# Two later starts: pieces six and seven of w_out are converted at slices 40 and 48 of the first product

## The chip, the cores and the metric

The kernel runs on one core of a Trainium2 chip. Its engines are TensorE (PE; its weight loads are PEld), VectorE (DVE), ScalarE (ACT), GpSimd (POOL) and SyncE (SP), which only issues transfers here. Each engine works through its own instructions in the order in which the program emits them. The metric is the device time of one execution in microseconds; lower is better.

## The reference, cut to what matters

Three stages follow each other for 2 batches of 768 tokens:

```python
# 1: retention, 8 heads of 64
state = gamma * state + k_t v_t^T ;  y_t = scale * q_t @ state
# 2: a gated feed-forward block, d_model 512, d_ff 1024
h = np.maximum(x @ w_in, 0.0)
conv_out = sum(conv_w[k] * hp[:, k:k + S, :] for k in range(3))
x = h * sigmoid(conv_out) @ w_out
# 3: eight experts, one for each token, chosen from logits
logits = x @ w_gate ;  out = p[e] * (relu(x @ w1[e]) @ w2[e])
```

All weights and activations of stage 2 count as float32, but `w_in`, `w_out` and `conv_w` arrive as 64-bit floats. The kernel reads them as pairs of 32-bit words and builds the float32 values itself.

## The kernel before, in words

**Precision.** A float32 product is done as three TensorE products in the faster fp32r form (`mm3`, lines 133 to 135): high part by high part, high by low, low by high. Each operand is therefore split into a high and a low part first.

**Conversion of a weight piece** (`convert`, line 160, with `narrow`, line 146). The matrix w_in comes in eight pieces of 128 x 512 and w_out in eight more, numbered m = 0 to 7. Called wo6 and wo7 here are the last two. One piece goes through these steps:

- SP issues the load of the raw words (line 143), long before the rest.
- DVE shifts and masks the high words (line 149, `na<-raw`) and merges two bits (line 150); ACT scales the low words (line 151, `raw<-raw`).
- POOL adds the two as integers (line 153, `na<-na,raw`).
- ACT writes the high part (line 174, `woh`), DVE the low part (line 176, `wol`).
- For w_out alone: TensorE turns the piece (line 185, `wt_ps`), ACT copies it (line 189, `wt`), TensorE multiplies it with the gate weights (line 193, `wc_ps`, only 9 columns wide), ACT stores that (line 195, `wc`).

`convert` is a generator. Each `yield n` says after how many further calls of `advance()` (line 409) it goes on, so it spreads over the work around it. A piece with an entry in `GATES` (line 157) waits ahead of its narrowing until the counter `slices[0]` has reached the entry.

**The product with w_in.** `stream(0, range(8))` emits, for each of eight blocks m of 128 features and each half u of the tokens, four slices of one `mm3` each (`ffn_in`, line 364): 64 slices, numbered from 0, so slices 0 to 7 are block 0, slices 32 to 39 block 4, slices 40 to 47 block 5. Its sum stands in a PSUM bank, `h_ps`, 128 x 384. After the fourth slice ACT applies the relu into a buffer `h` (line 376), which frees the bank. Slices 0 to 19 lie between chunks of stage 1; for slices 20 to 63 one `advance()` runs per slice:

```python
    psa = pool("psa", 3, q_stack, space=PSUM)
    ...
    for _ in first:
        slices[0] += 1
        advance()
```

That pool of three banks, handed out in turn, serves `h_ps` and from here on also `wc_ps`. So a `wc_ps` or an `h_ps` waits until the bank handed out three requests earlier has been read by ACT.

**The block chain** (`hidden`, line 346). A finished block m then goes, at fixed distances in slices (`TIMES`, line 381), through ACT `cc<-h,cw` (line 350), two DVE taps (line 353), the ACT sigmoid (line 355), a DVE product (line 357), the ACT high part `hg` (line 326), the DVE low part (line 330), and TensorE's logit products (`lg`, line 344), which also need the stored `wc` of the piece with the same number. Below, h3 is the chain of block 3, and so on.

The order of every engine's queue thus follows from these counts. ACT, for example, meets the relu of a block only after all that was emitted before it, whatever that waits for.

**Afterwards** batch 1 takes the same product, then the products with w_out (`x_ps`), the routing, and the experts with their weight loads; these stages use what was converted above.

Of the kernel before, what the change touches and what calls it, by code (L numbers as in the profile page):

```python
# [91 lines left out]
def tile_kernel(ctx, tc, cat, cst, qT, kT, kN, vN, w_in, conv_w, w_out, wg, w1, w2, out):  # L92
# [61 lines left out]
        yield 2  # L154
        return a.bitcast(F32)

    GATES, slices = {6: 34, 7: 44}, [0]
    turning, held, loaded, ready, banks = [], [], [], [], [0]

    def convert(src, hi, lo, m=None):  # L160
# [902 lines left out]
```

## Time and profile before

| what | value |
|---|---|
| runs shown, device us | 436.66, 432.30, 436.14; median 436.14 |
| profiled execution: device time | 432.95 us |
| profiled execution: span | 431.2 us |
| granted TensorE clock, mean | 0.99 of full speed |
| busy: PE, DVE, ACT, POOL | 95%, 67%, 60%, 21% of the span |
| PE busy, 85 to 135 us | 48.20 of 50.00 us, granted clock 0.97 |
| PE busy, 135 to 250 us | 112.23 of 115.00 us, granted clock 1.00 |

The span runs from the first to the last instruction. Matmuls are pipelined, so one lasts longer than the distance to the next one; distances between starts say what a stretch of TensorE work costs. A releaser in square brackets is the instruction whose end ended a wait.

### The profile page before, as it was taken

The numbers are of one execution on the slowest core, as the hardware profiler recorded it, in microseconds if no ns is written. First come the engines' busy times: TensorE is split into PE (matmuls) and PEld (weight loads), VectorE is DVE, ScalarE is ACT, GpSimd is POOL, SyncE is SP. The second block draws the span as 40 slices with busy tenths as digits, with TensorE's granted clock in tenths as the row PEclk, the third lists the DMA queues.
The fourth block names the chain that finished last, engine by engine and source line by source line (L and its number), as shares of the span: only waits on it lengthen the run. The fifth ranks groups of instructions, "written<-read, shape, count | busy, mean of one in ns | idle before, by whom it ended". The sixth has DMA issues, their size and how long they took to land.

```text
span 431.2 us, 7291 instructions
## 1 busy us (share of the span) xinstructions
PE 408.8 (95%) x2412; PEld 329.2 (76%) x2412; DVE 289.6 (67%) x518; ACT 259.2 (60%) x429; POOL 91.5 (21%) x92
## 2 busy tenths in 40 slices
PE   8898999999899999999999999999999999999991
PEld 7787897899798778988768776867738677776880
DVE  3798789787767260377899058968664796858650
ACT  2787677667666212566704166869556686958560
POOL 5256664211110000000000330305203132211210
PEclk9999999999899999999999999999999999999997
DMA  7989763230000101000197899999969999774100
GB/s 229 388 291 398 260 211 92 93 97 1 2 0 2 49 26 49 26 0 2 58 377 254 304 373 379 342 390 409 398 254 340 407 364 346 280 260 186 44 25 29
DMA packets 27324, 86.59 MB, mean 201 GB/s; under 512 B 3598, under 2 KB 4622, under 8 KB 27280
## 3 DMA queue, kind: packets, MB, share of 16 engines
q1 hardware_dynamic: 25200, 79.76, 50.4%
q0 software_dynamic: 2080, 6.29, 3.9%
q8 instruction: 21, 0.34, 0.3%
q14 instruction: 23, 0.19, 0.1%
HBM read 105.18 MB, written 6.55 MB: 259 GB/s over the span
## 4 chain that ended last, share of the span: by engine, by line
PE 35%; issue 26%; DMA 15%; DVE 14%; ACT 4%; POOL 3%; SPq 1%; POOLq 0%; DVEq 0%; ACTq 0%
DMA out_dram<-yo,it 13%; PE h_ps L133 5%; PE h_ps L134 4%; PE h_ps L135 4%; PE x_ps L133 4%; PE x_ps L134 3%; PE x_ps L135 3%; PE y L300 3%; DVE cc L353 3%; PE s_ps L282 2%; POOL xg L727 2%; PE inc L290 1%; DMA kq<-in_qT_dram 1%; PE y L302 1%; DVE na L149 1%
## 5 line engine op out<-in xcount | busy, mean ns | idle before, releaser
L133 PE MATMUL h_ps<-xT,wih 128*128 128x384 f32 x128 | 46.9, 366 | 0.0
L353 DVE SCALAR_TENSOR_TENSOR cc<-h,cw,cc 128x768 f32<-128x768 f32 x32 | 34.4, 1075 | 18.6 <-ACT cc L350 18.5
L863 POOL DMA_INDIRECT out_dram<-yo,it x13 | 16.7, 1282 | 136.3 <-ACT yo L862 136.3
L727 POOL DMA_INDIRECT xg<-xs,it x13 | 18.8, 1444 | 123.4 <-DMA qc<-in_w_dram 115.8
L134 PE MATMUL h_ps<-xT,wih 128*128 128x384 f32 x128 | 43.5, 340 | 0.0
L135 PE MATMUL h_ps<-xT,wil 128*128 128x384 f32 x128 | 43.4, 339 | 0.0
L133 PE MATMUL x_ps<-woh,hg 128*128 128x512 f32 x96 | 38.5, 401 | 0.0
L134 PE MATMUL x_ps<-wol,hg 128*128 128x512 f32 x96 | 37.6, 391 | 0.0
L135 PE MATMUL x_ps<-woh,hg 128*128 128x512 f32 x96 | 37.5, 391 | 0.0
L718 DVE TENSOR_TENSOR ws0l<-r,ws0l 128x1024 fp32r<-128x1024 f32 x22 | 26.0, 1221 | 16.3 <-ACT ws0l L717 16.2
L153 POOL TENSOR_TENSOR na<-na,raw 128x512 int32<-128x512 int32 (+1 forms) x17 | 21.9, 1289 | 48.9 <-ACT raw L151 17.7
L300 PE MATMUL y<-at,vz 128*128 128x128 f32 x192 | 30.6, 281 | 1.8 <-ACT vz L277 0.9
L718 DVE TENSOR_TENSOR ws0h<-r,ws0h 128x1024 fp32r<-128x1024 f32 x22 | 26.0, 1221 | 8.2 <-ACT ws0h L717 8.2
L718 DVE TENSOR_TENSOR wc<-r,wc 128x1024 fp32r<-128x1024 f32 x22 | 25.9, 1221 | 8.0 <-ACT wc L717 8.0
L717 ACT ACTIVATE ws0l<-r 128x1024 fp32r<-128x1024 f32 x22 | 22.1, 1052 | 13.9 <-PE y L135 13.9
L282 PE MATMUL s_ps<-qz,kq 128*128 128x256 f32 x96 | 29.2, 386 | 1.0 <-issue 1.0
L718 DVE TENSOR_TENSOR ws1h<-r,ws1h 128x1024 fp32r<-128x1024 f32 x22 | 26.0, 1221 | 6.0 <-ACT ws1h L717 3.8
L717 ACT ACTIVATE wc<-r 128x1024 fp32r<-128x1024 f32 x22 | 22.1, 1054 | 11.3 <-PE g L135 11.3
L300 PEld LDWEIGHTS y<-at,vz 128*128 128x128 f32 x192 | 25.4, 191 | 4.3 <-DVE xT L305 2.3
L284 DVE TENSOR_TENSOR at<-s_ps,ca 128x256 f32<-128x256 f32 x48 | 20.2, 420 | 11.7 <-PE s_ps L282 11.6
L133 PEld LDWEIGHTS h_ps<-xT,wih 128*128 128x128 f32 x128 | 24.6, 192 | 3.1 <-issue 1.8
L489 ACT ACTIVATE xn<-x_ps 128x512 f32<-128x512 f32 x10 | 6.0, 599 | 32.8 <-PE x_ps L135 18.2
(231 smaller groups left out, 1044.9 us busy)
## 6 DMA issues: line engine op xcount, KB each, us to landing
r<-in_w_dram SPq DMA_DIRECT2D x88, 512.0 KB
qc<-in_w_dram SPq DMA_DIRECT2D x32, 512.0 KB
qs1l<-in_w_dram SPq DMA_DIRECT2D x32, 512.0 KB
raw<-in_w_in_dram SPq DMA_DIRECT2D x8, 512.0 KB
raw<-in_w_out_dram SPq DMA_DIRECT2D x8, 512.0 KB
kq<-in_qT_dram SPq DMA_DIRECT2D x7, 384.0 KB
kq<-in_kT_dram SPq DMA_DIRECT2D x7, 384.0 KB
kv<-in_vN_dram SPq DMA_DIRECT2D x7, 384.0 KB
```

The source lines that it names most:

```text
L133: te.matmul(ps, lhi, rhi, start=first, stop=False)
L134: te.matmul(ps, lhi, rlo, start=False, stop=False)
L135: te.matmul(ps, llo, rhi, start=False, stop=last)
L153: po.tensor_tensor(out=a, in0=a, in1=lo, op=ALU.add)
L282: te.matmul(ps, self.kq[:, 0, tok], self.qz[:, :, tok], start=True, stop=True)
L284: ve.tensor_tensor(out=self.at[c], in0=ps, in1=self.dm, op=ALU.mult)
L300: te.matmul(y, vz[:, c, j, :], at[:, j, :], start=(j == 0), stop=(c == 0 and j == 1))
L353: ve.scalar_tensor_tensor(out=cc, in0=h[:, i:i + S], scalar=cw[:, m, i:i + 1], in1=cc, op0=ALU.mult, op1=ALU.add)
L717: se.activation(out=w[:, 0, h, :], in_=r, func=AF.Copy)
L718: ve.tensor_tensor(out=w[:, 1, h, :], in0=r, in1=w[:, 0, h, :].bitcast(F32), op=ALU.subtract)
L727: return po.indirect_dma_start(out=xg, out_offset=None, in_=xs[0:n], in_offset=bass.IndirectOffsetOnAxis(ap=it[:, j:j + 1], axis=0), bound ...
L863: po.indirect_dma_start(out=out, out_offset=bass.IndirectOffsetOnAxis(ap=it[:, j:j + 1], axis=0), in_=yo, in_offset=None, bounds_check=NT ...
```

## The change

One line is changed. It sets from which slice on pieces 6 and 7 of w_out may be narrowed; their loads, their steps and the number of calls between the steps are as they were.

```diff
-    GATES, slices = {6: 34, 7: 44}, [0]
+    GATES, slices = {6: 40, 7: 48}, [0]
```

The line that reads it, in `convert`, is unchanged:

```python
        while slices[0] < GATES.get(m, 0):
            yield 1
```

## Rows read from the trace of the kernel before

**Rows 1.** Chain of waits, 80 to 140 us: start, time (us), engine, tile, line.

```profile
105.69 0.43 DVE na L149
106.14 0.69 DVE na L150
106.84 0.87 DVE cc L357
107.70 1.98 DVE cc L353
109.71 0.84 ACT cc L355
110.55 0.52 ACT woh L174
111.07 0.39 ACT h L376
```

**Rows 2.** TensorE timeline: start, us, engine, line, operation, tiles, count [idle, releaser].

```profile
100.34 0.34 PE L135 MATMUL h_ps<-xT,wil 128*128 128x384 f32 x1
...
101.72 0.42 PE L133 MATMUL h_ps<-xT,wih 128*128 128x384 f32 x1
...
103.42 0.44 PE L133 MATMUL h_ps<-xT,wih 128*128 128x384 f32 x1
...
104.74 0.34 PE L134 MATMUL h_ps<-xT,wih 128*128 128x384 f32 x1
...
109.60 0.34 PE L135 MATMUL h_ps<-xT,wil 128*128 128x384 f32 x1
...
111.50 1.35 PE L193 MATMUL wc_ps<-wgs,wt 128*128 128x9 f32 x8 [1.57 <-ACT h L376]
...
113.46 0.67 PE L133 MATMUL h_ps<-xT,wih 128*128 128x384 f32 x1
...
115.71 0.34 PE L134 MATMUL h_ps<-xT,wih 128*128 128x384 f32 x1
...
130.56 0.45 PE L133 MATMUL h_ps<-xT,wih 128*128 128x384 f32 x1
```

**Rows 3.** Busy time by window: us; PE, PEld, DVE, ACT, POOL; granted clock; DMA.

```profile
110.00:111.40 1.40, 0.00 (x0) 0.00 (x0) 0.84 (x2) 1.40 (x3) 0.00 (x0) 1.00 0.00 0
111.40:113.40 2.00, 1.90 (x12) 1.90 (x13) 1.34 (x3) 1.23 (x4) 0.00 (x0) 0.68 0.00 0
113.40:115.50 2.10, 2.10 (x8) 2.10 (x8) 2.10 (x4) 0.60 (x1) 0.00 (x0) 0.50 0.00 0
120.00:131.00 11.00, 11.00 (x81) 9.89 (x80) 8.22 (x10) 7.49 (x14) 0.53 (x1) 1.00 0.01 1
```

**Rows 4.** DVE timeline, the first tap of h3 and a later product.

```profile
104.75 1.02 DVE L353 SCALAR_TENSOR_TENSOR cc<-h,cw,cc 128x768 f32<-128x768 f32 x1 [0.86 <-ACT cc L350]
...
122.70 0.95 DVE L357 TENSOR_TENSOR cc<-cc,h 128x768 f32<-128x768 f32 x1
```

**Rows 5.** POOL timeline, the adds of wo6 and of wo7.

```profile
107.09 1.76 POOL L153 TENSOR_TENSOR na<-na,raw 128x512 int32<-128x512 int32 x1 [8.13 <-DVE na L150]
118.13 1.51 POOL L153 TENSOR_TENSOR na<-na,raw 128x512 int32<-128x512 int32 x1 [9.27 <-ACT raw L151]
```

**Rows 6.** Groups by line, 102 to 131 us: busy us, mean ns; idle, releasers.

```profile
L330 DVE TENSOR_TENSOR hg<-cc,hg 128x768 fp32r<-128x768 f32 x5 | 4.8, 955 | 1.2 <-ACT hg L326 1.2
L376 ACT ACTIVATE h<-h_ps 128x384 f32<-128x384 f32 x9 | 4.3, 482 | 4.0 <-PE h_ps L135 4.0
L326 ACT ACTIVATE hg<-cc 128x768 fp32r<-128x768 f32 x5 | 4.2, 844 | 3.9 <-DVE cc L357 3.9
L350 ACT ACTIVATE cc<-h,cw 128x768 f32<-128x768 f32 x4 | 3.7, 933 | 0.1
L189 ACT ACTIVATE wt<-wt_ps 128x512 f32<-128x512 f32 x4 | 2.2, 586 | 0.8 <-PE wt_ps L185 0.8
L151 ACT ACTIVATE raw<-raw 128x512 int32<-128x512 uint32 x2 | 1.3, 674 | 0.0
```

## The prediction

> **What bounds the kernel now.** I read the profile from the whole to the place. The table above says that TensorE is busy 95% of the span, and nearly all the time in the stage that the change touches. So only a hole in TensorE's work there can be worth anything. The waits of TensorE show one hole of size in that stage: the gate product `wc_ps` of piece wo5 sat idle 1.57 us until a relu on ACT had ended [rows 2]. That product needs a PSUM bank; the relu that frees it is that of the second half of block 4.
>
> The chain of waits says why the relu came so late [rows 1]. Read it downward: DVE narrows wo6 (0.43 and 0.69), then does the product of h2, then the second tap of h3, which took 1.98 where a tap alone takes 1.02 [rows 4]; then comes ACT's sigmoid of h3, then the high part of wo6, and only then the relu, at 111.07. The long tap lies beside POOL's add for wo6, from 107.09 to 108.85 [rows 5]. So three things of wo6 stand ahead of one relu: its narrowing, its add, and its high part. They stand there because the gate opens at slice 34, while the relu belongs to slice 39.
>
> The windows show what the hole did afterwards [rows 3]. TensorE does nothing from 110.0 to 111.4, at a granted clock of 1.00. The stretch behind it has 0.68, and the next one, to 115.5, has 0.50, the lower of the two levels (1.2 GHz). From 120 to 131 us TensorE is busy for 11.00 of 11.00 us at 1.00 again. Thus the hole costs twice.
>
> **What the hole costs, from distances** [rows 2]. From the last product of slice 40 to the first of slice 41 lie 113.46 - 109.60 = 3.86 us; in between are one `wc_ps` block and one `wt_ps` block. The same sequence took 101.72 - 100.34 = 1.38 us ten microseconds earlier. Excess: 2.48. The next seven steps took 115.71 - 113.46 = 2.25 us against 104.74 - 103.42 = 1.32. Excess: 0.93. Together 3.41 us.
>
> **The change, part by part.** It removes and adds no instruction. Two pieces move, wo6 by six slices and wo7 by four, each with its two DVE narrowing steps, ACT scaling, POOL add, ACT high part, DVE low part, and the TensorE and ACT steps behind them.
>
> *Queues.* SP issues both loads ahead of the gate, at the same places as before, so no transfer moves. On POOL, nothing lies between the two adds; behind them follows the clearing of a buffer of the last stage. So both cost nothing.
>
> *Does the old hole close?* Without wo6 in the way, h2's product follows h3's first tap at 105.77 [rows 4]. It ends at 106.72 (0.95), the second tap at 107.74 (1.02), the sigmoid at 108.58 (0.84), the relu at 109.06 (0.48, [rows 6]). TensorE asks for the bank one step after 109.60, about 109.8. The relu is early by 0.7 us, with nothing counted for the overlap of neighbouring instructions (on the chain a relu takes 0.39, not 0.48). So I give the full 3.41 us back, the clock's share included: without the hole I see no reason for the clock to fall.
>
> *wo6 in its new place.* ACT scales the words right behind that relu, until 109.73 (0.67); DVE ends its steps at about 109.8 (107.74 + 0.96 for h2's low part + 0.43 + 0.69). The add runs 1.5 to 1.8 us [rows 5], to 111.6 at worst. It will hold the first tap of h4, ready at 110.66, as it held h3's. By the old pattern a tap ends 0.83 us after the add, here 112.4, some 0.7 late. The relu of block 5's first half is ahead of all that in ACT's queue. The second half's relu comes behind the sigmoid of h4, at about 115.2 instead of 115.0; its bank is next wanted by wo6's `wc_ps` near 119.6. Cost: nothing, hidden by 4 us of slack.
>
> *wo7 in its new place.* Here it is tighter. ACT has the relu (115.7), wo6's `wt` copy (0.59, to 116.3) and wo7's scaling (to 117.0) in a row. The add ends between 118.5 and 118.8, or up to 0.6 sooner with overlap. TensorE asks for it, to turn wo7, at about 110.6 + 13 slices of 0.55 + 0.9 = 118.65 (a slice is three steps of 1.32/7, a little less behind its first; 0.9 is an estimate for one turn and one block of logits, from the 1.2 us of a `wc_ps` block and a turn in the undisturbed stretch). So it waits 0 to 0.2.
>
> The tap of h5 is held until 119.6, its chain's product and second tap end at 121.6, the sigmoid at 122.4, and the relu of block 6's second half at 122.9; TensorE wants that bank at slice 60, near 123.8. Then come the copy, `cc` of h6 (0.93), a tap and the product of h5, which is ready at 126.6 without overlap and 125.9 with it. TensorE comes to the logits of h5 at about 126.7 (slice 64 starts at 130.56 - 3.41 = 127.15). The same again, half a microsecond worse, at the logits of h6. No row shows how these small margins fall. Bounds: 0 if all overlap, 1.5 us if none does. I take 0.2, near the first end, since the chain's durations [rows 1] are the overlapped ones.
>
> *The sum:* 3.41 - 0.2 = 3.2 us less, between 1.9 and 3.5. The profiled execution would go from 432.95 to 429.75. That execution lies 3.19 below the median of the runs shown, and those lie up to 4.36 apart; against the median the forecast is 436.14 - 3.2 = **432.9 us**. Nothing behind this stage gives it back: no transfer there is tied to a fixed time, so all of it starts earlier.
>
> **Where a rule speaks against it.** The rows show an add and a tap that lengthen each other, 1.76 and 1.98 us [rows 1, 5]. The Trainium skill, page SBUF — State Buffer, section "Who interferes with whom", says that a VectorE instruction with two SBUF inputs and a GpSimd instruction that reads SBUF exclude each other, and that whichever was issued first keeps the shared ports to its end. The trace agrees with it (1.98 against 1.02). By it the order of issue decides, and that could come out the other way for wo7, which is the first rival.
>
> **The rivals.**
>
> *The hole moves to the turn of wo7 (no change).* If h5's first tap gets in ahead of wo7's add, the add begins at the tap's end, 117.9 + 1.02 = 118.9, and ends at 120.4 (1.51). TensorE then waits 1.8 us at the turn, about as long as in the old hole, and with the same fall of the clock the 3.41 us are spent again: 436.1. For it: the add and h5's tap are released by neighbouring ACT instructions. Against it: the scaling that releases the add stands 0.93 us ahead of the `cc` that releases the tap. Also in this case falls that the gate decides nothing, being open before the piece is ready; the chain speaks against it, since wo6's narrowing stands right ahead of h2's product, where slice 34 puts it [rows 1]. Chance 0.20.
>
> *DVE runs late at the logits (slower).* The chains of h5, h6 and h7 now carry wo7 with them and TensorE no longer pauses for DVE to catch up. If the product of h5 is later than I have it by 1.8 us or more, TensorE stops at the logits of h5 and, the chain being the same, at those of h6. Two holes like the old one cost 2 x 3.41 for 3.41 saved: 436.14 + 3.41 = 439.6. One such hole is the point from which it is no gain, two from which it is a loss. Against it: DVE is busy only 8.22 of the 11 us from 120 on [rows 3]. Chance 0.10.
>
> **How the numbers follow.** Forecast 0.70, the rivals 0.20 and 0.10. The range runs from 428.5 (the fastest run shown, 432.30, less 3.5, rounded down) to 437.2 (the slowest, 436.66, plus half a microsecond, in the case of no change). That leaves out the slower case and some of the tails. One per cent, about what a measurement of this kernel can tell from no change, is 4.4 us; my gain of 3.2 is 0.7%. So even the forecast is mostly "within 1%": I split it 0.26 faster, 0.44 same. The no-change case gives 0.16 same and 0.02 on either side, the slower case 0.08 slower and 0.02 same. Sum: faster 0.28, same 0.62, slower 0.10.
>
> **What would show it right or wrong.** In the changed kernel's trace: no idle time of `wc_ps` for a relu near 110 us; the second tap of h3 at 1.02 us; a granted clock of 1.00 from 107 to 131 us; slice 64 starting near 127.2 to 127.5. POOL's adds should start near 109.8 and 117. Wrong would be a hole ahead of `wt_ps` of wo7 near 118.6, at slice 60, or ahead of the logits of h5 or h6; or a stage that is shorter by 3 us while the experts end no earlier.

## The result and the profile after

The changed kernel is faster by a little less than one per cent: the ratio to the kernel before is **0.9914, 95% interval 0.9893 to 0.9936**. The medians are 430.76 us (18 runs, 427.92 to 433.30) and, timed beside it, 434.39 us (18 runs). The profiled execution took 429.99 us with a span of 428.2. All ratios here leave out a kernel's runs that lie more than 1.5% above its fastest; the profiled run of e9 below is such a run.

First the windows of TensorE's stage, the same stretches as [rows 3] and then the whole of it (columns: window, us, busy PE, PEld, DVE, ACT, POOL, granted clock, DMA share, GB/s).

```profile
110.00:111.40 1.40, 1.40 (x15) 1.40 (x12) 1.25 (x3) 1.40 (x4) 0.00 (x0) 1.00 0.04 12
111.40:113.40 2.00, 2.00 (x16) 2.00 (x15) 1.44 (x1) 0.76 (x3) 1.29 (x1) 1.00 0.00 0
113.40:115.50 2.10, 2.10 (x16) 2.07 (x15) 2.10 (x4) 1.35 (x3) 0.00 (x0) 1.00 0.00 0
120.00:131.00 11.00, 11.00 (x81) 9.87 (x80) 8.70 (x12) 7.38 (x13) 0.53 (x1) 1.00 0.01 1
...
107.00:131.00 24.00, 24.00 (x171) 21.72 (x170) 19.94 (x25) 17.34 (x31) 3.14 (x3) 1.00 0.00 1
```

TensorE is busy for all 24 us and the clock is 1.00 throughout; the 1.40 us of nothing and the stretch at 0.50 are gone.

TensorE's timeline of the changed kernel, to be laid beside [rows 2].

```profile
110.87 0.42 PE L133 MATMUL h_ps<-xT,wih 128*128 128x384 f32 x1
...
111.30 0.34 PE L135 MATMUL h_ps<-xT,wil 128*128 128x384 f32 x1
111.48 0.95 PE L193 MATMUL wc_ps<-wgs,wt 128*128 128x9 f32 x8
112.29 0.42 PE L133 MATMUL h_ps<-xT,wih 128*128 128x384 f32 x1
...
120.26 0.60 PE L185 MATMUL wt_ps<-cs,na 128*128 128x128 f32 x4
...
128.91 0.45 PE L133 MATMUL h_ps<-xT,wih 128*128 128x384 f32 x1
```

The gate product of wo5 starts 0.18 us behind the last product of slice 40, where it was 1.90 (111.50 - 109.60, [rows 2]). From here on I measure the **stretch** from the first product of slice 40 to the first of slice 64, which holds the same TensorE work in every kernel (but for the products added in e4): 128.91 - 110.87 = 18.04 us. Before it was 130.56 - 109.16 = 21.40; the row at 109.16 is this one, from the same timeline of the kernel before.

```profile
109.16 0.42 PE L133 MATMUL h_ps<-xT,wih 128*128 128x384 f32 x1
```

So the stage gives 3.36 us. The profiled spans differ by 3.0: this execution reached slice 40 1.71 us later, and needed 1.35 less behind slice 64. Neither can be laid to the change: over all traces of this document slice 40 starts between 108.69 and 111.11 us, and what lies behind slice 64 takes between 298.8 and 304.3 us, whatever the gates.

DVE, ACT and POOL of the changed kernel around the old hole and in the new places (timelines).

```profile
108.26 1.01 DVE L353 SCALAR_TENSOR_TENSOR cc<-h,cw,cc 128x768 f32<-128x768 f32 x1
...
111.96 1.69 DVE L353 SCALAR_TENSOR_TENSOR cc<-h,cw,cc 128x768 f32<-128x768 f32 x1 [0.68 <-ACT cc L350]
...
119.07 1.36 DVE L353 SCALAR_TENSOR_TENSOR cc<-h,cw,cc 128x768 f32<-128x768 f32 x1 [1.01 <-ACT cc L350]
```
```profile
110.06 0.47 ACT L376 ACTIVATE h<-h_ps 128x384 f32<-128x384 f32 x1
```
```profile
111.54 1.29 POOL L153 TENSOR_TENSOR na<-na,raw 128x512 int32<-128x512 int32 x1 [10.88 <-DVE na L150]
118.29 1.32 POOL L153 TENSOR_TENSOR na<-na,raw 128x512 int32<-128x512 int32 x1 [5.45 <-ACT raw L151]
```

The second tap of h3 takes 1.01 us, where it took 1.98 by the chain [rows 1] and 2.05 by the timeline. The relu of block 4 starts 0.81 us ahead of slice 40 (110.06 against 110.87); before, it started behind it. The two adds now lengthen the first taps of h4 and h5 instead, to 1.69 and 1.36, and nobody on TensorE waits for those. The add of wo7 ends at 119.61 (118.29 + 1.32), 0.65 us ahead of the turn of wo7 at 120.26.

### The profile page after: what moved, and what is told of

The parts are those of the page before. It is cut to its first block, busy times and chain, and to the rows that moved or that the text cites. A ratio compares the mean times of both kernels' runs of the same rounds, so it can differ in the third digit from the quotient of the medians.

```text
span 428.2 us, 7291 instructions
## 1 busy us (share of the span) xinstructions
PE 407.2 (95%) x2412; PEld 328.1 (77%) x2412; DVE 289.5 (68%) x518; ACT 259.1 (61%) x429; POOL 90.8 (21%) x92
## 4 chain that ended last, share of the span: by engine, by line
PE 40%; issue 26%; DMA 16%; DVE 11%; ACT 3%; POOL 2%; SPq 1%; POOLq 0%; DVEq 0%; ACTq 0%
DMA out_dram<-yo,it 14%; PE h_ps L133 6%; PE h_ps L134 5%; PE h_ps L135 5%; PE x_ps L133 4%; PE y L300 3%; PE x_ps L135 3%; PE x_ps L134 3%; PE s_ps L282 3%; PE wc_ps L193 2%; PE inc L290 2%; DMA kq<-in_qT_dram 2%; PE lg L344 1%; PE y L302 1%; DVE cc L353 1%
## 5 line engine op out<-in xcount | busy, mean ns | idle before, releaser
L304 ACT ACTIVATE xT<-y 128x128 fp32r<-128x128 f32 x48 | 13.2, 274 | 20.9 <-PE y L302 19.0
```

## The experiments

The stretch, the longest idle time of TensorE in it, the lowest clock behind that and the ratio to the kernel before, for all. A stretch is that of one execution; the changed kernel's came out at 18.04 twice.

| kernel | stretch, us | idle, us | clock | ratio, 95% interval |
|---|---|---|---|---|
| before | 21.40 | 1.57 | 0.50 | 1 |
| changed | 18.04 | none | 1.00 | 0.9914 [0.9893, 0.9936] |
| e1, wo6 alone | 18.57 | 0.27 | 1.00 | 0.9900 [0.9866, 0.9933] |
| e2, wo7 alone | 21.47 | 1.57 | 0.50 | 0.9995 [0.9959, 1.0032] |
| e3, own bank | 19.40 | 0.95 | 1.00 | 0.9937 [0.9905, 0.9969] |
| e4, hole filled | 19.81 | none | 1.00 | 0.9984 [0.9951, 1.0018] |
| e5, add emitted late | 20.92 | 1.06 | 0.50 | 0.9976 [0.9944, 1.0009] |
| e6, gates 44 and 52 | 22.30 | 2.23 | 0.50 | 1.0003 [0.9960, 1.0045] |
| e7, high part late | 20.94 | 1.05 | 0.50 | 0.9976 [0.9939, 1.0014] |
| e8, gates 36 and 48 | 18.07 | none | 1.00 | 0.9875 [0.9819, 0.9931] |
| e9, scaling late | 19.87 | 0.17 | 0.50 | 0.9925 [0.9895, 0.9954] |
| e10, changed again | 18.04 | none | 1.00 | 0.9915 [0.9885, 0.9945] |
| e11, gates 36 and 48 again | 18.08 | none | 1.00 | 0.9871 [0.9829, 0.9913] |
| e12, scaling late again | 18.32 | 0.17 | 1.00 | 0.9929 [0.9895, 0.9964] |

The 0.17 of e9 and e12 is the distance to the next product less the usual 0.17.

**e1 and e2: which piece matters.**

```diff
-    GATES, slices = {6: 34, 7: 44}, [0]
+    GATES, slices = {6: 40, 7: 44}, [0]     # e1
+    GATES, slices = {6: 34, 7: 48}, [0]     # e2
```

> Only the gate of piece wo6 moves, from 34 to 40; wo7 stays at 44. Theory (the hole is made by wo6's narrowing, add and high part standing ahead of the relu of block 4): the hole at the gate product of wo5 is gone and the granted clock stays 1.00, so the whole gain of the change comes: about 3.4 us less than before in the stage, ratio 0.992. Rival (both moves are needed, because wo7 at 44 now follows wo6 at 40 too closely): a hole of 1 us or more ahead of the turn of wo7 or at the relu of block 5, ratio 0.996 to 1.000.

> Only the gate of piece wo7 moves, from 44 to 48; wo6 stays at 34. Theory: the hole at the gate product of wo5 stays as it was, 1.6 us idle, with the clock at 0.50 behind it; ratio 1.000. Rival (DVE and ACT are too full around slices 44 to 50, and it is wo7 that delays the relu): the hole shrinks by half or more, ratio 0.995 or less.

TensorE's timeline: e1 has no wait but a small one, at the turn of wo7; e2 has the old hole to the hundredth.

```profile
110.73 0.42 PE L133 MATMUL h_ps<-xT,wih 128*128 128x384 f32 x1
...
118.48 0.65 PE L185 MATMUL wt_ps<-cs,na 128*128 128x128 f32 x4 [0.27 <-POOL na L153]
...
129.30 0.45 PE L133 MATMUL h_ps<-xT,wih 128*128 128x384 f32 x1
```
```profile
113.46 1.36 PE L193 MATMUL wc_ps<-wgs,wt 128*128 128x9 f32 x8 [1.57 <-ACT h L376]
```

Moving wo6 is the change: alone it gives 2.83 of the 3.36 us (21.40 - 18.57). Moving wo7 alone is worth nothing; together with wo6 it saves a further 0.5 us of the stretch (18.57 - 18.04), which the times cannot tell. That wo6 matters and wo7 alone does not, the times show as well: the two intervals do not overlap.

**e3: a bank that nobody else wants.**

```diff
-        pg = (psg.tile(...) if len(banks) == 1 else psa.tile([P, 512], F32, tag="a", name="wc_ps"))[:, 0:E + 1]
+        pg = (psg.tile(...) if len(banks) == 1 else psb.tile([P, DM], F32, tag="x2", name="wc_ps"))[:, 0:E + 1]
```

> The gates stay at 34 and 44; the gate products of the w_out pieces take their bank in the last stretch from the pool that the products with w_out will use later, which is idle there, instead of the pool of three that they share with the product with w_in. Theory (the wait is for a bank that a relu of block 4 must free): the relu stays as late as before, near 111 us with the tap beside the add at 2 us, but TensorE doesn't wait for it: no hole, clock 1.00, 3.4 us less, ratio 0.992. Rival (TensorE needs the late ACT and DVE work anyway and only waits at the next place): the hole comes back at slice 44 or at the turn of wo6, ratio 0.997 to 1.000.

ACT's relu, DVE's long tap and TensorE of this kernel (timelines).

```profile
110.46 0.47 ACT L376 ACTIVATE h<-h_ps 128x384 f32<-128x384 f32 x1
```
```profile
107.11 2.05 DVE L353 SCALAR_TENSOR_TENSOR cc<-h,cw,cc 128x768 f32<-128x768 f32 x1
```
```profile
109.32 0.96 PE L193 MATMUL wc_ps<-wgs,wt 128*128 128x9 f32 x8
...
117.88 0.66 PE L185 MATMUL wt_ps<-cs,na 128*128 128x128 f32 x4 [0.95 <-POOL na L153]
...
121.89 0.53 PE L344 MATMUL lg<-cc,wc 128*32 128x192 f32 x8 [0.23 <-DVE cc L357]
```

The tap is as long (2.05) and the relu as late as before (110.46, 1.75 behind slice 40 at 108.71; before, 110.98 behind 109.16 by 1.82), yet the gate product of wo5 starts at once. So the wait was for the bank, and for nothing else. Both sides of the expectation had a part: of the 3.36 us 2.00 come back, and 1.36 are spent again, 0.95 of it idle at the turn of wo7; the rival had named other places for that. The work on DVE and ACT that delayed the relu is still ahead of wo7: its narrowing starts 5.96 us behind slice 40 here (114.67 against 108.71), where in e1, with wo6 out of the way and the same gate for wo7, it starts 4.51 behind (115.24 against 110.73).

**e4: the hole filled with work.**

```diff
+        if m == 5:
+            fill = psb.tile([P, DM], F32, tag="x2", name="fill")
+            for _ in range(7):
+                te.matmul(fill[:, 0:P], zst[0], zst[0], start=True, stop=True)
         pg = ...
```

> Gates as before; seven float32 products of 128 x 128 x 128 into an unused bank, about 1.5 us of TensorE work that nobody reads, stand ahead of the gate product of wo5 and so run while it waits for its bank. Theory (the low clock follows from the idle stretch and costs as much as the idle time itself): the relu comes no earlier, slice 41 starts within 0.5 us of where it did less the clock's share, the clock stays 1.00, and 1.7 us of the 3.4 come back: ratio 0.996. Rival (the clock falls because of the narrow products, not because of the idle stretch, or it costs next to nothing): clock near 0.5 again behind it, ratio 1.000.

TensorE's timeline and, below it, the windows of this kernel.

```profile
111.16 1.72 PE L194 MATMUL fill<-st 128*128 128x128 f32 x14
112.89 1.06 PE L197 MATMUL wc_ps<-wgs,wt 128*128 128x9 f32 x8
```
```profile
111.20:112.90 1.70, 1.69 (x16) 1.50 (x14) 1.14 (x2) 1.67 (x4) 0.00 (x0) 1.00 0.00 0
112.90:116.00 3.10, 3.10 (x22) 3.10 (x23) 2.44 (x4) 1.75 (x4) 0.00 (x0) 1.00 0.00 0
```

The filler takes just the length of the hole (112.89 - 111.16 = 1.73 us), the gate product starts no sooner for it (2.35 us behind slice 40, before 2.34), and the clock stays at 1.00. The stretch shrinks by 21.40 - 19.81 = 1.59 us: that is what the low clock cost, beside the 1.73 of the hole itself. The time does not show it by itself: the interval of 0.9984 holds both 1 and the expected 0.996.

**e5 and e7: which of wo6's three delays counts.** In e5 the wait stands in `narrow` ahead of POOL's add, in e7 in `convert` ahead of ACT's high part.

```diff
+        while slices[0] < until:                              # e5: until is 42 for wo6, 50 for wo7
+            yield 1
         po.tensor_tensor(out=a, in0=a, in1=lo, op=ALU.add)
...
+        while slices[0] < {6: 44, 7: 52}.get(m, 0):           # e7
+            yield 1
         se.activation(out=hi, in_=w, func=AF.Copy)
```

> Gates at 34 and 44 for the narrowing as before, but POOL's add and all behind it start for wo6 at slice 42 and for wo7 at 50, as in the changed kernel. So of the three things that stood ahead of the relu of block 4, DVE's narrowing (1.1 us) stays, and the lengthened tap (1.0) and the high part (0.5) go. Theory (the three add up in one chain): the relu comes about 1.5 us sooner than before, within 0.2 us of when TensorE asks; the hole is 0 to 0.3 us, the clock stays 1.00, the stretch from slice 40 to slice 64 is 18.0 to 18.4 us (before 21.40, changed 18.04). Rival (it is the narrowing on DVE that matters): a hole of 1 us or more, 19 us or more.

> Gates at 34 and 44 and the adds where they were; only ACT's high part and all behind it start later, at slice 44 for wo6 and at 52 for wo7. Theory: the narrowing and the lengthened tap still delay the relu of block 4, which comes only 0.5 us sooner; the hole is 1.0 to 1.2 us idle. The run with a bank of its own had 0.95 us idle at one place and kept the clock at 1.00, the kernel before fell to 0.50 behind 1.57; if the clock holds here, the stretch from slice 40 to slice 64 is about 19.1 us, if it falls, 20.5 to 20.9. Rival (the high part alone is what blocks the relu): no hole, 18.0 to 18.3.

POOL's timeline of e5, and its windows; then slice 40 and the relu of e7 (timelines of TensorE and ACT).

```profile
106.69 1.76 POOL L155 TENSOR_TENSOR na<-na,raw 128x512 int32<-128x512 int32 x1 [8.16 <-DVE na L150]
```
```profile
109.50:110.50 1.00, 0.03 (x1) 0.00 (x0) 0.65 (x1) 1.00 (x2) 0.00 (x0) 1.00 0.00 0
...
112.20:115.10 2.90, 2.90 (x10) 2.90 (x10) 2.87 (x5) 0.68 (x2) 0.00 (x0) 0.50 0.00 0
```
```profile
109.02 0.42 PE L133 MATMUL h_ps<-xT,wih 128*128 128x384 f32 x1
```
```profile
110.32 0.47 ACT L378 ACTIVATE h<-h_ps 128x384 f32<-128x384 f32 x1
```

e5 failed as an experiment, and is worth reading for that. I had the program emit the add six slices later (42 for 36, the gate and two), but POOL's queue was empty, so the add ran as soon as its inputs were there: 2.06 us ahead of slice 40 (106.69 against 108.75), just as before (107.09 against 109.16). Only the high part moved, so e5 was e7 twice. The rival's numbers came out (a hole of 1 us or more, 19 us or more), but they say nothing of the narrowing, since the long tap stayed as well. Both take 0.5 us off the relu's delay, as e7's expectation said (idle 1.06 and 1.05), and both leave the clock to fall as before: 20.92 is 18.04 + 1.22 of hole, taken by the distances (1.40 - 0.18), + 1.66 of low clock. Of my two cases for the clock in e7 the worse one came out, at 20.94 just above its 20.5 to 20.9.

**e9 and e12: the narrowing alone stays.** The wait of e5, but ahead of ACT's scaling, until slices 40 and 48. The add needs the scaled words, so now it does move.

```diff
+        while slices[0] < until:
+            yield 1
         se.activation(out=lo, in_=lo.bitcast(U32), func=AF.Copy, scale=2.0 ** -29)
```

> The two narrowing steps of DVE stay at slices 34 and 44 as before, but ACT's scaling of the low words waits until slice 40 for wo6 and 48 for wo7. POOL's add needs the scaled words, so this time it cannot start early, as it did in the run that only emitted it later. So the narrowing (1.1 us on DVE) stays ahead of the relu of block 4 and the lengthened tap and the high part go. Theory (three delays add up): the relu starts near 109.4 us where TensorE asks at 109.8 less what the whole trace is shifted by, so the hole is 0 to 0.3 us, the clock stays 1.00 and the stretch from slice 40 to slice 64 takes 18.0 to 18.5 us; ratio 0.992. Rival (the narrowing alone is enough): a hole of 0.8 us or more, 19 us or more, ratio 0.996 or more.

> The kernel whose scaling waits until slices 40 and 48, once more. In its first profile the hole at the gate product of wo5 was 0.17 us, yet the clock fell to 0.50 behind it and the stretch from slice 40 to slice 64 took 19.87 us; that execution was among the slowest of its runs (434.77 us, median 431.67). If the fall belongs to that execution, the stretch takes 18.2 to 18.3 us here, clock 1.00. If it belongs to the kernel, it is 19.7 to 20.0 again, and the clock's share of the gain does not hang on the length of the hole.

TensorE and the relu of e9 (timelines), then TensorE of e12.

```profile
108.69 0.42 PE L133 MATMUL h_ps<-xT,wih 128*128 128x384 f32 x1
...
109.13 0.34 PE L135 MATMUL h_ps<-xT,wil 128*128 128x384 f32 x1
109.47 1.06 PE L195 MATMUL wc_ps<-wgs,wt 128*128 128x9 f32 x8
```
```profile
108.94 0.47 ACT L378 ACTIVATE h<-h_ps 128x384 f32<-128x384 f32 x1
```
```profile
109.64 0.34 PE L135 MATMUL h_ps<-xT,wil 128*128 128x384 f32 x1
109.99 1.06 PE L195 MATMUL wc_ps<-wgs,wt 128*128 128x9 f32 x8
```

The windows around the gate product of wo5 and a later one of e9, then those of e12.

```profile
109.40:110.40 1.00, 0.99 (x10) 0.93 (x9) 0.00 (x0) 1.00 (x3) 0.30 (x1) 1.00 0.00 0
...
111.00:112.00 1.00, 1.00 (x5) 1.00 (x4) 1.00 (x1) 0.00 (x0) 0.40 (x1) 0.50 0.00 0
...
210.00:250.00 40.00, 35.64 (x175) 29.30 (x174) 23.45 (x83) 8.47 (x13) 5.86 (x7) 0.92 0.83 298
```
```profile
108.00:110.40 2.40, 2.39 (x23) 1.78 (x15) 1.62 (x2) 2.32 (x5) 0.00 (x0) 1.00 0.03 7
...
111.00:114.00 3.00, 3.00 (x21) 2.97 (x20) 2.66 (x3) 1.29 (x5) 0.92 (x1) 1.00 0.00 0
```

The hole is 0.17 us in both, as the sum of the three delays says: the narrowing's 1.1 us is a little more than the relu can bear. Against the start of slice 40 the relu starts 1.82 us behind in the kernel before, 1.30 behind in e7 (110.32 - 109.02), 0.25 behind in e9 (108.94 - 108.69) and 0.81 ahead in the changed kernel. So the high part is worth 0.52, the long tap 1.05 and the narrowing 1.06, together the 2.63 by which the relu moved. The clock fell in one execution and not in the other, of one and the same kernel. The execution in which it fell was the longest of its twelve, 434.77 us with a median of 431.67, and its clock was low elsewhere too (0.92 from 210 to 250 us). So a hole of 0.17 us does not by itself make the clock fall: as far as two executions can tell, the fall belongs to the one execution, and e9's 19.87 is not the kernel's.

**e6: later still.** Gates 44 and 52.

> Both gates later still, 44 and 52. Theory (the gain is the hole's, and nothing more is to be had in this stage): the stretch from slice 40 to slice 64 is 18.0 to 18.2 us, as in the changed kernel, clock 1.00, ratio 0.992. Rival (later is worse, since wo7's last steps run past slice 64 and delay what follows): the same stretch, but 0.5 us or more lost between slice 64 and the products with w_out, ratio 0.995 or more.

TensorE and POOL of e6 (timelines), and a window behind the hole.

```profile
108.98 0.42 PE L133 MATMUL h_ps<-xT,wih 128*128 128x384 f32 x1
...
123.72 0.66 PE L185 MATMUL wt_ps<-cs,na 128*128 128x128 f32 x4 [2.23 <-POOL na L153]
...
131.28 0.42 PE L133 MATMUL h_ps<-xT,wih 128*128 128x384 f32 x1
```
```profile
121.90 1.77 POOL L153 TENSOR_TENSOR na<-na,raw 128x512 int32<-128x512 int32 x1 [6.25 <-DVE na L150]
```
```profile
125.40:128.90 3.50, 3.50 (x14) 3.50 (x14) 3.50 (x5) 1.68 (x4) 0.53 (x1) 0.52 0.00 0
```

Both sides missed on the stretch, and the rival's ratio came true for another reason. The hole at the gate product is gone, and another stands at the turn of wo7, for POOL's add, 2.23 us long and with the clock at 0.52 behind it, the edges of the window included (0.50 from 126 to 127 us). The whole gain is spent: ratio 1.0003, and a stretch that is 0.90 longer than before. The turn follows the gate by six slices, about 3.3 us of TensorE's time. In those wo7's narrowing must come through DVE behind the second tap of h5, its scaling through ACT, and then its add; all of that ended at 123.67 (121.90 + 1.77).

**e8, e10, e11: two slices instead of six.** Gates 36 and 48 (e8, e11), and the changed kernel beside it (e10).

> Gates at 36 and 48. At 36 the narrowing of wo6 comes right behind the second tap of h3 on DVE, and its high part, four slices later, right behind the relu of block 4 on ACT: nothing of wo6 is ahead of that relu any more, though the piece is only two slices later than before. Theory (what counts is the place in the queues, not the six slices): no hole at the gate product of wo5, clock 1.00, the stretch from slice 40 to slice 64 within 0.4 us of the changed kernel's 18.04; a small wait at the turn of wo6 or wo7 may remain. Rival (DVE and ACT need the later slices because they are too full around 107 to 111 us): a hole of 0.8 us or more, 19 us or more.

> The changed kernel once more, gates 40 and 48, beside the one with gates 36 and 48: 18.0 us from slice 40 to slice 64, ratio 0.991 to 0.992. If gate 36 is really better, this one is above it by 0.3% or more; if not, the two are alike.

> Gates 36 and 48 once more, since its first timing had 4 runs only. Its stretch from slice 40 to slice 64 was 18.07 us, the changed kernel's 18.04, so by the theory the two are alike, ratio 0.991 to 0.992; the ratio of 0.9875 seen first would then be scatter. Rival (it gains somewhere else): 0.9885 or less, and a stretch of the trace that is shorter.

DVE's timeline of e8: the narrowing now follows the second tap of h3.

```profile
105.42 0.95 DVE L357 TENSOR_TENSOR cc<-cc,h 128x768 f32<-128x768 f32 x1
106.28 1.01 DVE L353 SCALAR_TENSOR_TENSOR cc<-h,cw,cc 128x768 f32<-128x768 f32 x1
107.21 0.42 DVE L149 TENSOR_SCALAR na<-raw 128x512 int32<-128x512 int32 x1
107.67 0.69 DVE L150 SCALAR_TENSOR_TENSOR na<-raw,na 128x512 int32<-128x512 int32 x1
```

Two slices are as good as six for the stretch: 18.07 and 18.08 against 18.04. It is the place in DVE's and ACT's queues that counts. In time the kernel with gate 36 came out at 0.9875 and 0.9871, the changed one at 0.9914 and 0.9915. That is above gate 36 by more than the 0.3% that I had named as the sign that gate 36 is really better, and 0.9871 is below the rival's 0.9885. But e8 has 4 runs and e11 has 6, the intervals overlap, and the traces show no stretch that is shorter: the stage is the same, and the spans are 427.1 and 428.4 us against 428.2 and 425.7. Whether gate 36 gains something elsewhere stays open.

## Why the prediction was right

**The bound and the old hole: right.** The chain of waits named the right instruction and the right cause. e2 keeps the hole while wo7 moves, e1 loses it while wo6 alone moves, and e3 shows that the bank was the only thing waited for.

**What the hole costs: right.** I had 3.41 us from the distances; the stretch lost 3.36. Of its two shares, e4 gives the clock's as 1.59, where the distances leave 3.41 - 1.73 = 1.68.

**Does it close: right.** I had the relu end at 109.06 with slice 40 at 109.16, 0.10 ahead of it; it ended 0.34 ahead (110.06 + 0.47 against 110.87), since neighbours overlap. That wo6's narrowing, long tap and high part all delay the relu, and add up, e7, e9 and e12 show: 1.06, 1.05 and 0.52 us.

**The new places: right in direction, too dear in size.** I had the adds at 109.8 and 117.0. Less the shift of 1.71 they started at 109.83 and 116.58, and took 1.29 and 1.32, not 1.5 to 1.8, because no DVE instruction of two inputs was running as they began. The add of wo7 ended 0.65 us ahead of the turn, where I had a wait of 0 to 0.2. So the term for the small margins, 0.2 us within bounds of 0 and 1.5, measured 0. The taps of h4 and h5 were held 0.67 and 0.34 (1.69 and 1.36 less 1.02), not a whole add.

**The sum: right, a little low.** I had 3.2 us, 0.7%; the times give 0.86% (0.64 to 1.07). The median of 430.76 lies 2.1 below my 432.9; 1.75 of that is the kernel before, whose median in these runs was 434.39 and not 436.14. That the effect would stay within one per cent was right; that one per cent is about what can be told from no change was too cautious, since the interval of the 18 runs leaves 1 out. The range, 428.5 to 437.2, held the case of no change as well, so that the time lies in it says little; the stretch of 18.04 us bears the account. That the profiled execution, forecast at 429.75, took 429.99 is in part luck: the stage gave more than the 3.2, and the rest of that execution happened to take 0.36 us more (1.71 - 1.35).

**The rivals.** The first did not happen here, but e6 shows it: a hole at the turn of wo7, for POOL's add, that costs at least as much as the old one, and a ratio of 1.0003, which is the price that I gave. It comes from a narrowing that starts too late for the turn. The condition that I gave, a tap ahead of the add, is not the one that e6 shows. The second, DVE late at the logits, shows as a wait in e3 alone (0.23 us at the logits of h4). That the gate decides nothing is refuted by e1 and e8.

## What to carry to other kernels

Where the engine that bounds a stage waits once, look for what stands ahead of its releaser in that engine's queue, not at how busy the queue is: here two slices of delay, enough to fall behind one relu, did what six do. An instruction emitted later is only later if something is ahead of it in its queue or its inputs come later; on an idle engine, move the inputs. Moving work back has an end as well: with wo6 ten and wo7 eight slices later than before, the same kernel had a new hole at least as dear as the old one.

## What the runs showed of the hardware

A short hole can cost as much again in TensorE's clock, and the length of the hole alone does not say whether it will. Behind 1.57 us of idle time ahead of a gate product of 9 columns (kernel before, e2) the granted clock fell to 0.50 (1.2 GHz), and behind 1.06 and 1.05 us at the same place (e5, e7); each time some 1.6 us were lost on top. Behind 2.23 us ahead of a turn it fell as well (e6). In e3, 0.95 us ahead of a turn left it at 1.00, and so did 1.56 us among the products of stage 1 in the kernel before (timeline and window).

```profile
33.22 0.46 PE L290 MATMUL inc<-kv 128*128 128x128 f32 x2 [1.56 <-DVE st L297]
```
```profile
30.00:40.00 10.00, 8.24 (x58) 7.03 (x57) 9.25 (x29) 7.05 (x20) 6.33 (x6) 1.00 1.00 383
```

Each of these is seen in one execution of its kernel, and what decides is open. Filling the hole with products that nobody reads kept the clock at 1.00 (e4).

POOL's add and a DVE instruction of two inputs lengthen each other, and both orders are in these runs. The add takes 1.29 to 1.32 us where no such instruction is running as it starts, and 1.45 to 1.80 where one is (1.76 in e5). The tap that comes during an add takes 1.36 to 2.06 us, alone 1.02. This agrees with the page of the Trainium skill named ahead of the result (SBUF — State Buffer, section "Who interferes with whom"), by which the two exclude each other.
